# Attention and bilinear FFN on one core: later batches' q·kv as block-diagonal full-array products, dummy products spread over the first batch, g turned later

## The chip, the cores and the metric

One core of one Trainium2 chip. The metric is the device time of one execution in microseconds (us). Every run also has a span (first to last instruction in the trace) and a mean granted clock of TensorE. The time is the span plus 1.8 us (for example 330.38 and 328.6). A difference of under 2% counts as "same". Ratios are the mean time of one kernel's fast runs over that of the other's of the same rounds, so they are not quite the ratio of the medians that are quoted beside them. I call an execution near its kernel's lowest time a *good draw*, and one 1.4 us or more above it a *bad draw*.

Engines: PE is TensorE (products), PEld its weight loads, DVE is VectorE, ACT is ScalarE, POOL is GpSimd, SP is SyncE.

## The reference

```python
# q, k, v: (batch 8, heads 8, seq 576, dim 64), fp32
kv  = einsum('bhsd,bhse->bhde', k, v)          # 64x64 per head
o   = einsum('bhsd,bhde->bhse', q, kv)
x   = o / sqrt(mean(o*o, -1) + 1e-6) * g_norm  # then (4608 tokens) x 512
out = ((x @ w_a) * (x @ w_b)) @ w_out          # w_a, w_b: 512x1536, w_out: 1536x512
```

## The kernel before

The FFN works on strips of 512 tokens: 12 units of eight 128x128x512 products (four with w_a, four with w_b), then four output blocks of twelve products. This is the bulk of TensorE's work. The attention of batch b+1 is put into *slots* between the units of strip b. Batch 0 has nothing to hide behind and runs first, pair of heads by pair of heads, with dummy products of zeros to keep TensorE busy. Two heads (64 rows each) share the 128 partitions.

```python
    def kv(self, p, o):                     # two heads: halves of the columns
        for c in range(EC):                 # EC = 6 pieces of 96 tokens
            for j in range(2):
                nc.tensor.matmul(o[j * D : (j + 1) * D, :],
                    lhsT=kt[..][:, self.head(p, j), c, :], rhs=vt[..][:, self.head(p, j), c, :], ...)

    def head(self, p, j):                   # later batches pair head p with head p + 4
        return 2 * p + j if self.b < EARLY else p + j * NP

    def x(self, m, h, i0):                  # later batches: four 64x64 products, all quadrants
        ts = slice(h * HF, (h + 1) * HF)    # HF = 288 tokens
        for j, c in ((0, 0), (1, 1), (0, 1), (1, 0)):
            r = slice(j * D, (j + 1) * D)
            nc.tensor.matmul(P[c * D : (c + 1) * D, i0 + j, 0:HF],
                lhsT=self.kvs[r, 2 * m + c, :], rhs=self.qT[r, 2 * m + c, ts], ...)
        nc.scalar.activation(sq[(2 * m + h) % 3], P[:, i0 : i0 + 2, 0:HF], AF.Square)

    # ss: two products ones (128x128) x sq (288 columns), ACT rsqrt, DVE writes xt
    ...
    # the first batch
    dummy(10, 0)                            # 128x128x512 products of zeros
    A.qtr(0, 2)                             # transposes of q on TensorE
    A.qtr_out(0, 2)
    nc.tensor.matmul(P[:, 6, 0:1], lhsT=g_row, rhs=one, start=True, stop=True)
    nc.vector.tensor_copy(g_col, P[:, 6, 0:1])
    dummy(2, 7)
    A.kv1(0, 3)
    A.kv1_out(0, 3, nc.vector.tensor_copy)
    for p in range(NP - 1):
        A.qtr(p + 1, ..)                    # next pair's transposes
        A.qtr_out(p + 1, ..)
        if p: A.pst(p - 1, ..)              # DVE: xt of the pair before
        A.px(p, i)                          # q.kv, quadrants on the diagonal
        A.psq(p, i)                         # ACT: square
        A.kv1(p + 1, ..)
        dummy(1, 7)
        A.pss(p, SS)                        # sum of squares, ACT: rsqrt
        A.kv1_out(p + 1, ..)
    ...
    # slots: in each strip four x, each followed one unit later by its ss
```

## Time and profile before

| | before |
|---|---|
| time, first three timed runs | 327.41 us median (327.39 to 327.51) |
| the profiled execution | 330.38 us, span 328.6 |
| PE busy | 320.3 us, 97% of the span |
| x slots | 6 batches x 4 |

The profiled execution is 3 us slower than the timed ones.

The page of the kernel before, its first parts. PEclk is the granted clock in tenths, one digit for each fortieth of the span:

```profile
span 328.6 us, 4913 instructions
PE 320.3 (97%) x1962; PEld 148.4 (45%) x1997; DVE 123.6 (38%) x213; ACT 122.5 (37%) x206; POOL 60.0 (18%) x82
...
PEclk9999999999999999999999999999999999999999
...
PE 95%; DMA 2%; issue 1%; DVE 1%; ACT 1%; ACTq 0%
```

TensorE is what ends last (95% of the chain of waits). ACT and DVE have more than half their time free.

The PE timeline of before around one x slot. Columns: start in us, length in us, engine, line, operation, operands, rows and columns of the array, columns streamed, count:

```profile
66.95 1.03 PE L260 MATMUL P<-xt,wb_t 128*128 128x512 bf16 x4
67.91 0.32 PE L219 MATMUL P<-qT,kvs 64*64 64x288 bf16 x4
68.16 1.04 PE L260 MATMUL P<-xt,wa_t 128*128 128x512 bf16 x4
69.03 1.03 PE L260 MATMUL P<-xt,wb_t 128*128 128x512 bf16 x4
69.89 0.41 PE L231 MATMUL P<-sq,ones 128*128 128x288 bf16 x2
70.14 1.03 PE L260 MATMUL P<-xt,wa_t 128*128 128x512 bf16 x4
```

Lengths include the pipeline, so read starts. Undisturbed, four products of 512 columns take 0.863 us, 0.2158 each. From 66.95 to 69.03 there are eight of them (1.73 us) in 2.08 us: the x slot between them costs 0.35 us. From 69.03 to 70.14 there are four (0.86) in 1.11: the sum-of-squares slot costs 0.25 us, though it streams twice 288 columns where the four quadrants, all started within 10 ns, stream 288 once.

The PE timeline of before in the first batch:

```profile
1.19 4.45 PE L329 MATMUL P<-zeros 128*128 128x512 bf16 x10 [1.19 <-DVE eps_t L344]
...
9.15 0.69 PE L164 MATMUL P<-ident,qt 96*64 96x96 bf16 x12 [0.32 <-DVE kvs L158]
...
11.87 0.69 PE L164 MATMUL P<-ident,qt 96*64 96x96 bf16 x12
...
14.59 0.69 PE L164 MATMUL P<-ident,qt 96*64 96x96 bf16 x12
...
17.95 0.38 PE L260 MATMUL P<-xt,wa_t 128*128 128x512 bf16 x1 [0.16 <-issue]
...
19.19 0.38 PE L260 MATMUL P<-xt,wa_t 128*128 128x512 bf16 x1 [0.30 <-DVE xt L205]
```

Ten dummies in 4.45 us are 0.427 apart, double the 0.2158 of later: TensorE is at half rate. The clock's own record says so too: it has full rate from 17.456 us for 310.613 us, and nothing before. (310.613 is 91 times 3.413 us; that length is called a *window* below.) The row PEclk of the page still shows 9 in its first slices; stretches without a record read as full there. A pair of heads takes 2.72 us (9.15, 11.87, 14.59).

### The profile page before, as it was taken

How to read it: one execution, taken by the hardware profiler on the slowest of the kernel's cores; microseconds unless marked ns; L12 is line 12 of the kernel's file. 1: busy time of each engine (PE TensorE's matmuls, PEld its weight loads, DVE VectorE, ACT ScalarE, POOL GpSimd, SP SyncE). 2: the span in 40 equal slices, each digit the busy share in tenths (PEclk: the TensorE clock that was granted, in tenths of full speed). 3: DMA queues.
4: the chain of work that ended last, by engine and by line, in shares of the span. 5: the costliest groups of instructions: out<-in, count | busy, mean ns of one | idle time of the engine just before them, and what ended most of it. 6: DMA issues, size and time to landing. Idle time of an engine off the chain costs nothing.

```text
span 328.6 us, 4913 instructions
## 1 busy us (share of the span) xinstructions
PE 320.3 (97%) x1962; PEld 148.4 (45%) x1997; DVE 123.6 (38%) x213; ACT 122.5 (37%) x206; POOL 60.0 (18%) x82
## 2 busy tenths in 40 slices
PE   7999999999999999999999999999999999999995
PEld 3544454444444444444444444444444444444443
DVE  2453325444234432443245323642345234304421
ACT  3353234444234433553254324532354243223310
POOL 8945860410014050410060000000000000000000
PEclk9999999999999999999999999999999999999999
DMA  8999999791359999693599032002000200021002
GB/s 179 197 196 200 200 195 236 100 171 27 98 104 132 157 125 223 84 171 87 145 62 156 34 110 60 0 21 92 17 0 2 96 32 3 0 97 33 0 32 96
DMA packets 70043, 32.61 MB, mean 99 GB/s; under 512 B 43652, under 2 KB 65540, under 8 KB 70020
## 3 DMA queue, kind: packets, MB, share of 16 engines
q0 software_dynamic: 49712, 18.44, 47.4%
q1 hardware_dynamic: 19952, 13.50, 16.0%
q10 hardware_dynamic: 356, 0.36, 0.4%
q8 instruction: 15, 0.25, 0.3%
q14 instruction: 8, 0.07, 0.1%
HBM read 37.75 MB, written 12.98 MB: 154 GB/s over the span
## 4 chain that ended last, share of the span: by engine, by line
PE 95%; DMA 2%; issue 1%; DVE 1%; ACT 1%; ACTq 0%
PE P L260 57%; PE P L304 28%; PE P L142 2%; PE P L219 2%; PE P L231 2%; DMA g_row<-in_g_norm_dram 1%; PE P L164 1%; PE P L178 1%; PE P L191 1%; PE P L329 1%; DMA out_dram<-osb 1%; DVE xt L205 0%; ACT rs L195 0%; DVE osb L319 0%; ACT sq L187 0%
## 5 line engine op out<-in xcount | busy, mean ns | idle before, releaser
L276 DVE TENSOR_TENSOR ab<-P,asb 128x512 bf16<-128x512 f32 x108 | 74.5, 691 | 126.6 <-PE P L260 125.7
L260 PE MATMUL P<-xt,wb_t 128*128 128x512 bf16 x430 | 111.4, 379 | 0.4
L260 PE MATMUL P<-xt,wa_t 128*128 128x512 bf16 x410 | 109.6, 380 | 1.3 <-DVE xt L205 0.3
L304 PE MATMUL P<-wo_t,ab 128*128 128x512 bf16 (+1 forms) x434 | 97.1, 373 | 0.7 <-issue 0.3
L274 ACT CAST asb<-P 128x512 bf16<-128x512 f32 x108 | 63.0, 585 | 88.5 <-PE P L260 87.7
L260 PEld LDWEIGHTS <-wb_t 128*128 128x128 bf16 x432 | 42.3, 98 | 51.3 <-issue 0.5
L304 PEld LDWEIGHTS <-ab 128*128 128x128 bf16 x444 | 42.3, 98 | 46.2 <-issue 0.2
L260 PEld LDWEIGHTS <-wa_t 128*128 128x128 bf16 x432 | 40.1, 98 | 44.9 <-issue 0.2
L239 DVE SCALAR_TENSOR_TENSOR xt<-P,g_col,rs 128x288 bf16<-128x288 f32 x48 | 22.6, 513 | 19.6 <-ACT rs L234 19.6
L317 ACT COPY osb<-P 128x512 f32<-128x512 f32 x17 | 10.0, 585 | 49.3 <-PE P L304 47.5
L319 DVE COPY osb<-P 128x512 f32<-128x512 f32 x18 | 12.4, 692 | 33.0 <-PE P L304 33.0
L234 ACT ACTIVATE rs<-P,eps_t 128x576 f32<-128x576 f32 x24 | 17.8, 741 | 16.6 <-PE P L231 16.6
L226 ACT ACTIVATE sq<-P 128x576 bf16<-128x576 f32 x24 | 15.6, 651 | 18.3 <-PE P L219 18.3
L118 POOL DMA_DIRECT2D qs<-in_q_dram x12 | 19.3, 1819 | 2.0 <-issue 1.9
L115 POOL COPY gate<-qT 1x1 bf16<-1x1 bf16 x5 | 0.9, 176 | 98.0 <-DMA qT<-qs 98.0
L95 POOL DMA_DIRECT2D vt<-in_v_dram x13 | 14.7, 1132 | 0.9 <-DMA qt<-in_q_dram 0.6
L95 POOL DMA_DIRECT2D kt<-in_k_dram x13 | 14.8, 1142 | 0.1
L142 PEld LDWEIGHTS <-kt 96*64 96x64 bf16 x384 | 8.1, 117 | 6.4 <-issue 6.4
L205 DVE SCALAR_TENSOR_TENSOR xt<-P,g_col,rs 128x288 bf16<-128x288 f32 x16 | 7.6, 513 | 6.8 <-ACT rs L195 6.8
L142 PE MATMUL P<-vt,kt 96*64 96x64 bf16 x384 | 10.0, 203 | 0.0
L231 PE MATMUL P<-sq,ones 128*128 128x288 bf16 x48 | 9.8, 286 | 0.0
L195 ACT ACTIVATE rs<-P,eps_t 128x576 f32<-128x576 f32 (+1 forms) x9 | 6.2, 687 | 6.9 <-PE P L191 6.9
(47 smaller groups left out, 85.4 us busy)
## 6 DMA issues: line engine op xcount, KB each, us to landing
out_dram<-osb SPq DMA_DIRECT2D x23, 256.0 KB, 2.0
qs<-in_q_dram POOLq DMA_DIRECT2D x12, 288.0 KB, 7.5
kt<-in_k_dram POOLq DMA_DIRECT2D x6, 576.0 KB, 10.2
vt<-in_v_dram POOLq DMA_DIRECT2D x6, 576.0 KB, 12.6
out_dram<-osb SPq DMA_DIRECT2D x13, 128.0 KB, 2.3
wo_t<-in_moe_w_out_dram POOLq DMA_DIRECT2D x12, 128.0 KB, 6.0
wa_t<-in_moe_w_a_dram POOLq DMA_DIRECT2D x5, 256.0 KB, 9.1
wb_t<-in_moe_w_b_dram POOLq DMA_DIRECT2D x5, 256.0 KB, 9.7
```

What stands on the lines that cost most here:

```text
L95: nc.gpsimd.dma_start(out=t[:, hs, :, :], in_=src[b, hs].rearrange("h (t c) d -> t h c d", c=EC))
L118: nc.gpsimd.dma_start(out=d[:, :, j, :], in_=q[b, j * NP : (j + 1) * NP].rearrange("h t d -> t h d"),)
L142: nc.tensor.matmul(o[j * D : (j + 1) * D, :], lhsT=kt[self.b % NB][:, self.head(p, j), c, :], rhs=vt[self.b % NB][:, self.head(p, j), c, : ...
L226: nc.scalar.activation(sq[(2 * m + h) % 3], P[:, i0 : i0 + 2, 0:HF], AF.Square)
L231: nc.tensor.matmul(P[:, i0 + j, 0:HF], lhsT=ones, rhs=sq[n][:, j, :], start=True, stop=True)
L234: nc.scalar.activation(rs[n], P[:, i0 : i0 + 2, 0:HF], AF.Abs_reciprocal_sqrt, bias=eps_t)
L239: nc.vector.scalar_tensor_tensor(out=xt[m + 2 * j][:, t0 : t0 + HF], in0=P[:, x0 + j, 0:HF], scalar=g_col, in1=rs[n][:, j, :], op0=ALU.mul ...
L260: nc.tensor.matmul(self.a if w is wa_t else self.b, lhsT=w[:, kc, self.fc * 128 : (self.fc + 1) * 128], rhs=xt[kc][:, t0 : t0 + STRIP], st ...
L274: nc.scalar.copy(self.t, self.a)
L276: nc.vector.tensor_mul(abt[self.s % 2][self.fc], self.b, self.t)
L304: nc.tensor.matmul(P[:, i, e0:e1], lhsT=abt[s % 2][fc][:, g * 128 : (g + 1) * 128], rhs=wo_t[:, fc, e0:e1], start=(fc == 0), stop=(fc == F ...
L319: nc.vector.tensor_copy(t, P[:, i, :])
```

## The change

The intent, in two halves. In later batches, two heads' kv (64x64 each) go on the diagonal of a 128x128 tile whose other two blocks are zero; one product of 128 rows then gives both heads, without switching the array to 64x64 tiles. Heads 2p and 2p+1 are now paired throughout, which changes how q is laid down. In the first batch, 11 and 4 dummies instead of 10 and 2 run before the first kv, five more are spread over the loop, and g is turned into a column after the first x instead of before the first kv.

```diff
+    kvb = [sb([128, NP, 128], BF16, f"kvb{i}") for i in range(2)]   # zeroed once by DVE
...
-        d = qs_d[b].rearrange("t (p j d) -> t p j d", p=NP, j=2)
-        for j in range(2): ... d[:, :, j, :] <- q[b, j * NP : (j + 1) * NP]
+        d = qs_d[b].rearrange("t (h d) -> t h d", h=H)
+        for hs in (slice(0, NP), slice(NP, H)): ... d[:, hs, :] <- q[b, hs]
...
-        def kv_out(self, p0, p1, src):
-            nc.scalar.copy(self.kvs[:, p0:p1, :], src)
+        def kv_out(self, src):
+            for j in range(2):
+                r = slice(j * D, (j + 1) * D)
+                nc.scalar.copy(kvb[self.b % 2][r, :, r], src[r])
...
-        def x(self, m, h, i0):  ... four 64x64 products (above)
+        def x(self, p, i0):
+            for h in range(2):
+                nc.tensor.matmul(P[:, i0 + h, 0:HF], lhsT=kvb[self.b % 2][:, p, :],
+                    rhs=self.qT[:, p, h * HF : (h + 1) * HF], start=True, stop=True)
...
-    dummy(10, 0)
+    dummy(11, 0)
     A.qtr(0, 2)
     A.qtr_out(0, 2)
-    nc.tensor.matmul(P[:, 6, 0:1], lhsT=g_row, rhs=one, start=True, stop=True)
-    nc.vector.tensor_copy(g_col, P[:, 6, 0:1])
-    dummy(2, 7)
+    dummy(4, 7)
...                                          # in the loop over pairs
         A.psq(p, i)
+        if p == 0:
+            nc.tensor.matmul(P[:, 1, 0:1], lhsT=g_row, rhs=one, start=True, stop=True)
+            nc.vector.tensor_copy(g_col, P[:, 1, 0:1])
+        dummy(1, 2 + p % 2)
         A.kv1(p + 1, 2 + p % 2)
         dummy(1, 7)
         A.pss(p, SS)
         A.kv1_out(p + 1, 2 + p % 2, nc.vector.tensor_copy)
+        if p < NP - 2:
+            dummy(1, 2 + (p + 1) % 2)
```

More of the change, by code (lines that the diff above doesn't have):

```diff
@@ L115, in load_late @@
             nc.gpsimd.tensor_copy(gate, qT[(b - 1) % 2][0:1, 0, 0:1])
-        d = qs_d[b].rearrange("t (p j d) -> t p j d", p=NP, j=2)
-        for j in range(2):
-            nc.gpsimd.dma_start(
-                out=d[:, :, j, :],
-                in_=q[b, j * NP : (j + 1) * NP].rearrange("h t d -> t h d"),
-            )
+        d = qs_d[b].rearrange("t (h d) -> t h d", h=H)
+        for hs in (slice(0, NP), slice(NP, H)):
+            nc.gpsimd.dma_start(out=d[:, hs, :], in_=q[b, hs].rearrange("h t d -> t h d"))
         load_heads(b, kt[b % NB], k, slice(0, H))
@@ L133, in __init__ @@
             self.qT = qT[b % 2]
-        def head(self, p, j):
-            return 2 * p + j if self.b < EARLY else p + j * NP
         def kv(self, p, o):
@@ L143, in kv @@
                         o[j * D : (j + 1) * D, :],
-                        lhsT=kt[self.b % NB][:, self.head(p, j), c, :],
-                        rhs=vt[self.b % NB][:, self.head(p, j), c, :],
+                        lhsT=kt[self.b % NB][:, 2 * p + j, c, :],
+                        rhs=vt[self.b % NB][:, 2 * p + j, c, :],
                         start=(c == 0),
@@ L165, in qtr @@
                         t[j * D : (j + 1) * D, c, :],
-                        qt[self.b][:, self.head(p, j), c, :],
+                        qt[self.b][:, 2 * p + j, c, :],
                         ident[0:EP, 0:EP],
@@ L212, in pst @@
                 )
-        def x(self, m, h, i0):
-            ts = slice(h * HF, (h + 1) * HF)
-            for j, c in ((0, 0), (1, 1), (0, 1), (1, 0)):
-                r = slice(j * D, (j + 1) * D)
+        def x(self, p, i0):
+            for h in range(2):
                 nc.tensor.matmul(
-                    P[c * D : (c + 1) * D, i0 + j, 0:HF],
-                    lhsT=self.kvs[r, 2 * m + c, :],
-                    rhs=self.qT[r, 2 * m + c, ts],
+                    P[:, i0 + h, 0:HF],
+                    lhsT=kvb[self.b % 2][:, p, :],
+                    rhs=self.qT[:, p, h * HF : (h + 1) * HF],
                     start=True,
                     stop=True,
-                )
-            nc.scalar.activation(sq[(2 * m + h) % 3], P[:, i0 : i0 + 2, 0:HF], AF.Square)
-        def ss(self, m, h, i0, x0):
-            n = (2 * m + h) % 3
-            for j in range(2):
-                nc.tensor.matmul(
-                    P[:, i0 + j, 0:HF], lhsT=ones, rhs=sq[n][:, j, :], start=True, stop=True
-                )
-            nc.scalar.activation(
-                rs[n], P[:, i0 : i0 + 2, 0:HF], AF.Abs_reciprocal_sqrt, bias=eps_t
-            )
-            t0 = self.b * S + h * HF
-            for j in range(2):
-                nc.vector.scalar_tensor_tensor(
-                    out=xt[m + 2 * j][:, t0 : t0 + HF],
-                    in0=P[:, x0 + j, 0:HF],
-                    scalar=g_col,
-                    in1=rs[n][:, j, :],
-                    op0=ALU.mult,
-                    op1=ALU.mult,
                 )
@@ L347 @@
     nc.vector.memset(ones, 0.0)
+    for t in kvb:
+        nc.vector.memset(t, 0.0)
     nc.vector.memset(ones[0:D, 0:D], 1.0 / D)
@@ L447, in slot @@
             if n == k0 + kn - 1:
-                A.kv_out(0, NP, kb)
-        for i, (m, h) in enumerate(((0, 0), (1, 0), (0, 1), (1, 1))):
-            if n == xs[i]:
-                A.x(m, h, X[0])
-            if n == xs[i] + 1:
-                A.ss(m, h, SS, X[0])
+                A.kv_out(kb)
+        for p in range(NP):
+            if n == xs[p]:
+                A.x(p, X[0])
+                A.psq(p, X[0])
+            if n == xs[p] + 1:
+                A.pss(p, SS)
+                A.pst(p, X[0])
     for s in range(1, N_STRIP - 1):
```

## The prediction

> **What bounds the kernel now.** TensorE: busy 320.3 of 328.6 us in the engine table, 95% of the chain of waits. After the first batch, PE work is critical one for one. Two parts are touched.
>
> 1. Later batches (six, four x slots each). In the timeline at 67.9 us four 64x64 products of 288 columns start within 10 ns (all four quadrants at once), but the stream stops on both sides: last full product at 67.600, second one after the slot at 68.384. Less two steps of 0.216 that is 0.352 us a slot. The sum-of-squares slot, two full 128x128 products of 288 columns, steps by 0.122 us without a break: 0.247 us. The Trainium skill, "TensorEngine Tiling (Array Packing)", Key Properties, says a change of tiling mode drains TensorE; the trace agrees.
>
> 2. First batch (0 to 18 us). 512-column dummies step by 0.427 us until 17.2 us, later products by 0.216. The clock record of full speed starts at 17.456 us and lasts 310.613, 91 times 3.413. The Trainium skill, "TensorE: Matmul & The Clock Gate", Part 1, has a free-running window of 3413 ns that must be busy before TensorE leaves half rate. So the whole first batch runs at half rate, one pair per 2.72 us (transposes at 9.15, 11.87, 14.59 us).
>
> **What the change does.**
> - x: 16 quadrant products per batch become 8 full ones, shaped like the sum-of-squares ones. Estimate: 0.352 - 0.247 = 0.105 us, times 24 slots = -2.5 us, all on PE. ACT gets one more kv copy per batch (about 0.37 us) and has room (37% busy); DVE's two memsets fit before the first loads land. The new q layout should cost nothing.
> - Dummies: 11, the transposes and 4 more make 6.9 us of unbroken work from 1.19 us at half rate, over two windows, so one whole window fits at any phase. I expect full rate from about 7 us, kept by the dummies in the loop. Moving g takes about 0.5 us out of the path to the first kv.
> - At full rate the ACT chain sets the pair's period: square 0.65, rsqrt 0.74, and the turn over PE, about 0.6 to 0.7: 2.0 to 2.2 us. With the first x product 1 us earlier I estimate the dense part 2.3 us sooner. The loads cap it: batch 1's first k/v pair landed 3.7 us before its use.
>
> Sum: -2.5 - 2.3, about -4.8 us.
>
> **Prediction:** 322.6 us, 8 in 10 between 320.5 and 325.2. Faster by over 2% (below 320.9): 0.14; within 2%: 0.85; slower: 0.01.
>
> **What would show it.** (a) Each later x group: two products 0.12 us apart, no break around them; a strip's period from 34.6 to about 34.2 us. (b) The full-speed clock record begins near 7 us. (c) First-batch pairs every 2.1 us with PE waiting for ACT's square; the third unit's products (21.90 us before) begin near 19.5. (d) Little PE waiting on loads.
>
> **What would make it wrong.** Timed runs are 3 us below the profiled one, so before may already reach full rate earlier when timed; then the first batch gives little. Products of zeros may not count as activity: then five extra dummies in the loop cost about 2 us. Or the first batch gains over 3.7 us and then stalls on loads. Or x slots wait for DVE's buffer release, which already held one slot per strip (0.15 us at 77.74 us).

## The result, and the profile after

| | before | after |
|---|---|---|
| first measurement, median | 327.46 us (4 runs, 327.39 to 327.51) | 324.82 us (3 fast runs, 324.81 to 325.27); 325.04 with the run of 854.88 counted |
| ratio | | 0.9924, 95% interval 0.9905 to 0.9944 |
| measured again, median | 327.65 us (11 runs, 327.08 to 330.10) | 324.86 us (6 runs, 324.80 to 325.70) |
| ratio | | 0.9898, 0.9864 to 0.9931 |
| mean of those runs | 328.33 us | 325.04 us |

The change is faster by 0.8 to 1.0%, within the 2% that counts as the same. The range of the prediction held the result, but near its slow end: 2.6 us were won by the medians of fast runs (2.8 when measured again) and not 4.8. That is not the whole mechanism confirmed: one of the two terms of the sum is not in the timed runs at all, as shown below, and the range was wide enough to hold the result without it.

One of the four runs of the changed kernel in the first measurement took 854.88 us, and it was the profiled one. Products of 512 columns were 0.621 us apart in most cases and 0.485 in about one of five, neither the half nor the full rate seen elsewhere (the 0.587 of an expectation below is a mean over a stretch of them), and its clock table was empty. None of the other nine runs of this kernel did this. It is a slow run and explains nothing here; the profile below is of the changed kernel run again unaltered (run after_again, span 323.0).

The page of the changed kernel, in that repeat:

```profile
span 323.0 us, 4853 instructions
PE 316.9 (98%) x1957; PEld 150.9 (47%) x1957; DVE 124.1 (38%) x215; ACT 124.7 (39%) x212; POOL 60.2 (19%) x82
...
PE 96%; DMA 2%; DVE 1%; ACT 0%; issue 0%; ACTq 0%
```

Its PE timeline around the same x slot:

```profile
64.03 1.03 PE L234 MATMUL P<-xt,wb_t 128*128 128x512 bf16 x4
64.89 0.41 PE L214 MATMUL P<-qT,kvb 128*128 128x288 bf16 x2
65.14 1.03 PE L234 MATMUL P<-xt,wa_t 128*128 128x512 bf16 x4
66.00 1.03 PE L234 MATMUL P<-xt,wb_t 128*128 128x512 bf16 x4
```

Eight products of 512 columns and the slot now take 66.00 - 64.03 = 1.97 us: the slot costs 0.25 us, like the sum-of-squares slot, and the 0.1 us of silence ahead of it (67.81 to 67.91 before) is gone.

Its PE timeline in the first batch:

```profile
1.19 3.84 PE L303 MATMUL P<-zeros 128*128 128x512 bf16 x11 [1.19 <-DVE eps_t L318]
5.79 0.45 PE L161 MATMUL P<-ident,qt 96*64 96x96 bf16 x12 [0.76 <-DVE qt L344]
...
7.84 0.45 PE L161 MATMUL P<-ident,qt 96*64 96x96 bf16 x12 [0.32 <-DVE kvs L155]
...
10.30 0.45 PE L161 MATMUL P<-ident,qt 96*64 96x96 bf16 x12
...
12.45 0.45 PE L161 MATMUL P<-ident,qt 96*64 96x96 bf16 x12
...
16.26 0.38 PE L234 MATMUL P<-xt,wa_t 128*128 128x512 bf16 x1 [0.31 <-DVE xt L202]
16.48 0.38 PE L234 MATMUL P<-xt,wb_t 128*128 128x512 bf16 x1
...
18.98 1.03 PE L234 MATMUL P<-xt,wa_t 128*128 128x512 bf16 x4
```

Full rate begins at 3.853 us by the clock record, and the pairs take 2.46 and 2.15 us (7.84, 10.30, 12.45) instead of 2.72. The product that waits for DVE's xt stands at 16.26 us instead of 19.19. Against the profile of before this is 2.9 us sooner, the 2.3 us and more that was forecast. But the timed runs do not show it. So the two profiles do not compare what the timed runs compare.

### The profile page after: what moved, and what is told of

Same layout as the page of the kernel before. It is cut to its first block, busy times and chain, and to the rows that moved or that the text cites. A ratio compares the mean times of both kernels' runs of the same rounds, so it can differ in the third digit from the quotient of the medians.

```text
span 853.1 us, 4818 instructions
## 1 busy us (share of the span) xinstructions
PE 835.1 (98%) x1922; PEld 267.5 (31%) x1957; DVE 124.7 (15%) x215; ACT 126.0 (15%) x212; POOL 60.4 (7%) x82
## 4 chain that ended last, share of the span: by engine, by line
PE 96%; issue 2%; DMA 1%; POOL 0%; DVE 0%; ACT 0%; POOLq 0%
PE P L234 59%; PE P L278 30%; PE P L188 3%; PE P L214 2%; PE P L137 2%; DMA qt<-in_q_dram 1%; DMA wb_t<-in_moe_w_b_dram 1%; PE P L175 1%; PE P L161 0%; PE P L303 0%; POOL wa_t L331 0%; POOL vt L96 0%; DVE osb L473 0%; POOL ident masks.py:199 0%; ACT osb L471 0%
## 5 line engine op out<-in xcount | busy, mean ns | idle before, releaser
L234 PE MATMUL P<-xt,wb_t 128*128 128x512 bf16 x422 | 279.8, 834 | 3.4 <-issue 3.4
L234 PE MATMUL P<-xt,wa_t 128*128 128x512 bf16 x419 | 277.6, 834 | 5.2 <-issue 5.2
L278 PE MATMUL P<-wo_t,ab 128*128 128x512 bf16 (+1 forms) x434 | 258.9, 817 | 3.6 <-issue 3.6
L234 PEld LDWEIGHTS <-wb_t 128*128 128x128 bf16 x432 | 73.9, 171 | 181.6 <-issue 181.1
L278 PEld LDWEIGHTS <-ab 128*128 128x128 bf16 x444 | 77.0, 174 | 166.1 <-issue 163.2
L234 PEld LDWEIGHTS <-wa_t 128*128 128x128 bf16 x432 | 74.7, 175 | 156.0 <-issue 155.2
L192 ACT ACTIVATE rs<-P,eps_t 128x576 f32<-128x576 f32 (+1 forms) x33 | 24.0, 726 | 89.9 <-PE P L188 82.6
L188 PE MATMUL P<-sq,ones 128*128 128x288 bf16 x64 | 29.8, 582 | 0.0
L214 PE MATMUL P<-qT,kvb 128*128 128x288 bf16 x48 | 21.9, 579 | 0.0
L303 PE MATMUL P<-zeros 128*128 128x512 bf16 x21 | 13.2, 773 | 1.2 <-DVE eps_t L318 1.2
```

The source lines that it names most:

```text
L188: nc.tensor.matmul(P[:, i0 + h, 0:HF], lhsT=ones, rhs=sq[p % 3][:, h, :], start=True, stop=True)
L192: nc.scalar.activation(rs[p % 3][:, h0:h1, :], P[:, i0 + h0 : i0 + h1, 0:HF], AF.Abs_reciprocal_sqrt, bias=eps_t,)
L214: nc.tensor.matmul(P[:, i0 + h, 0:HF], lhsT=kvb[self.b % 2][:, p, :], rhs=self.qT[:, p, h * HF : (h + 1) * HF], start=True, stop=True,)
L234: nc.tensor.matmul(self.a if w is wa_t else self.b, lhsT=w[:, kc, self.fc * 128 : (self.fc + 1) * 128], rhs=xt[kc][:, t0 : t0 + STRIP], st ...
L278: nc.tensor.matmul(P[:, i, e0:e1], lhsT=abt[s % 2][fc][:, g * 128 : (g + 1) * 128], rhs=wo_t[:, fc, e0:e1], start=(fc == 0), stop=(fc == F ...
L303: nc.tensor.matmul(P[:, i, 0:cols], lhsT=zeros[:, 0:128], rhs=zeros[:, 0:cols], start=True, stop=True)
```

## The experiments

Twelve runs, all correct. Nine are in the table; the other three are more profiles of the kernel before.

| run | x | front (dummies, g) | dummies added in the loop | median us (range) | runs 1.5 us or more above the lowest | full rate from, in the profile |
|---|---|---|---|---|---|---|
| before_again | quadrants | 10, g, 2 | no | 328.42 (327.45 to 330.41) | 3 of 6 | 6.13 us |
| after_again | full | 11, 4, g later | yes | 324.86 (324.80 to 325.70) | 0 of 6 | 3.85 us |
| x_only | full | 10, g, 2 | no | 325.57 (324.69 to 327.11) | 3 of 6 | 6.48 us |
| first_only | quadrants | 11, 4, g later | yes | 327.50 (327.46 to 327.71) | 0 of 6 | 5.21 us |
| front_only | full | 11, 4, g later | no | 324.66 (324.45 to 324.74) | 0 of 6 | 4.07 us |
| loop_only | full | 10, g, 2 | yes | 325.60 (324.68 to 327.79) | 3 of 6 | 6.66 us |
| front_early | full | 11, 4, g later | no | 324.54 (324.51 to 324.70) | 0 of 6 | 4.98 us |
| quad_pairs | halves on the diagonal | 11, 4, g later | yes | 330.12 (330.00 to 330.42) | 0 of 6 | 4.63 us |
| no_dummies | full | none, g later | none at all | 327.36 (326.78 to 327.83) | 0 of 6 | 18.83 us |

The first four ran on one chip with 11 runs of before (327.08 to 330.10), front_only to quad_pairs on a second with 11 (327.40 to 330.38), no_dummies on a third with 11 (327.30 to 330.14).

Theory A: x pays all of the gain; the dummies bring full rate, but the timed runs of before mostly had it already. Theory B: the dummies pay, x does not.

### after_again, before_again: the two kernels unaltered

> The changed kernel unaltered, for a profile in the fast state (the one on hand shows TensorE stepping 512 columns every 0.587 us for the whole span, and 853 us). Theory A (the products pay, the dummies bring full rate but the timed runs of the kernel before already had it): each later x slot costs 0.247 us on the stream instead of 0.352, 2.5 us in all, and full rate begins near 7 us. Theory B (the dummies pay, the x slots do not): x slots still cost about 0.35 us. Ratio to before 0.992 either way.

> The kernel before unaltered, for a second profile. If the profiled execution on hand reached full rate late by chance of the window's phase, this one starts its full-rate record at another time (for example 10.6 or 14.0 us) with a span 1.5 to 3 us shorter than 328.6; if it is a property of the kernel, again near 17.5 us and 328.6. Ratio 1.000.

Ratio of after_again 0.9898 (0.9864 to 0.9931), of before_again 1.0009 (0.9967 to 1.0052). The profile of before_again has a span of 325.7 us, 2.9 us less than the first profile of the same kernel. Its PE timeline in the first batch:

```profile
1.20 4.45 PE L329 MATMUL P<-zeros 128*128 128x512 bf16 x10 [1.20 <-DVE eps_t L344]
...
7.90 0.45 PE L164 MATMUL P<-ident,qt 96*64 96x96 bf16 x12 [0.32 <-DVE kvs L158]
...
9.79 0.45 PE L164 MATMUL P<-ident,qt 96*64 96x96 bf16 x12
...
11.80 0.45 PE L164 MATMUL P<-ident,qt 96*64 96x96 bf16 x12
...
15.56 0.38 PE L260 MATMUL P<-xt,wa_t 128*128 128x512 bf16 x1 [0.26 <-DVE xt L205]
16.46 0.39 PE L260 MATMUL P<-xt,wb_t 128*128 128x512 bf16 x1 [0.52 <-DMA wb_t<-in_moe_w_b_dram]
...
18.98 1.03 PE L260 MATMUL P<-xt,wa_t 128*128 128x512 bf16 x4
```

Full rate from 6.128 us, pairs every 1.89 to 2.01 us, and then TensorE waits for the second w_b block, which landed at 16.41 us by the trace. The changed kernel's product with that block stands at 16.48 us. There the block landed at 16.39, but the wait that ended last was for DVE's xt, at 16.26; with an earlier xt that product could have come less than 0.1 us sooner before it met the load. The last lines of the two timelines settle it: the third unit of the first strip starts at 18.98 us in both. So in a good draw the first batch has next to nothing to give. The first profile of before was a bad draw.

### x_only, first_only: the change in two halves

The edits are the diff above, split: x_only takes everything but the lines of the first batch, first_only takes those alone.

> Only the full 128-row products in the later batches; the first batch is as in the kernel before. Theory A: 2.5 us faster than before, ratio 0.992, so the same as the whole change. Theory B: within 0.5 us of before. If both halves pay and something takes half back, about 2.5 us faster here and also faster in the other half.

> Only the spread dummies and the later g; x in quadrant products as before. Theory A: within 0.5 us of before, ratio 0.9985 to 1.0015, though the profile shows full rate from about 7 us. Theory B: 2.5 us faster. If products of zeros do not count as activity: full rate not before 17 us and 1 to 2 us slower.

x_only: ratio 0.9917 (0.9878 to 0.9956). first_only: 0.9973 (0.9938 to 1.0009). The full products win 327.50 - 324.86 = 2.64 us (first_only to after_again, medians, both without bad draws), which is 0.110 us for each of 24 slots; 0.105 was forecast. The good draws of x_only and of before in the same rounds say the same, 324.72 against 327.45 by their medians. The other half does not move the good runs (lowest 327.46, before's good runs 327.08 to 327.65) but it takes the bad draws away: three of six in x_only are 1.5 to 2.4 us above its lowest, none in first_only is more than 0.3. In means, 328.33 of before falls by 2.66 in x_only and by 0.80 in first_only, together 3.46; the whole change has 3.29. (The 0.80 alone is not clear of noise, the interval of first_only reaches 1.0009. That bad draws go with the front is clear only over all runs, see below.) Theory A stands and Theory B falls, but A's claim that first_only has no effect holds for the median only.

### front_only, loop_only: which dummies

```diff
# front_only, against the change
-        dummy(1, 2 + p % 2)
...
-        if p < NP - 2:
-            dummy(1, 2 + (p + 1) % 2)
# loop_only, against the change
-    dummy(11, 0)
+    dummy(10, 0)
...
-    dummy(4, 7)
+    nc.tensor.matmul(P[:, 6, 0:1], lhsT=g_row, rhs=one, start=True, stop=True)
+    nc.vector.tensor_copy(g_col, P[:, 6, 0:1])
+    dummy(2, 7)
...
-        if p == 0: (g, in the loop)
```

> The whole change without the five dummies inside the first batch's loop; the 11 and 4 in front and the later g stay. Each kernel so far has runs near its lowest time and, where the loop has no extra dummies, about half the runs 1.5 to 3 us above it. Theory F (the unbroken front brings full rate at any phase and that is enough): all runs within 1 us of 324.8. Theory L (the gaps inside the loop let TensorE fall back to half rate, whatever the front does): some of six runs at 326 to 327.5 with a mean granted clock below 0.995.

> The whole change with the front as before (10 dummies, g, 2 dummies) but the five dummies in the loop kept. Theory L: all runs within 1 us of 324.8. Theory F: some of six runs 1.5 us or more above that.

front_only: ratio 0.9868 (0.9833 to 0.9902), six runs within 0.29 us. loop_only: 0.9910 (0.9866 to 0.9955), with runs at 326.26, 327.64 and 327.79. Theory F holds: the unbroken front does it, and the added dummies in the loop protect nothing that shows. (One dummy a pair, which the kernel before has too, stays in both.) They may cost a little: front_only's median is 0.2 us below the change's, but on different chips, so this is not shown. Nor do the runs separate the three edits of the front, one dummy more, then two more, and g moved away.

### no_dummies: what the dummies are worth at all

```diff
# against front_only
-    dummy(11, 0)
-    dummy(4, 7)
-        dummy(1, 7)
```

> front_only without any dummy. If the front dummies are what brings full rate before the first batch, TensorE starts it at half rate in every run here: pairs about 2.3 to 2.7 us apart, full rate only when the dense first strip has filled a window, near 18 to 22 us, and all six runs 3 to 5 us above front_only (327.5 to 329.5), with none near 324.7. If the transposes and kv products were enough by themselves, within 0.5 us of 324.7.

Ratio 0.9965 (0.9931 to 0.9999); 2.70 us above front_only by the medians, on different chips, a little less than the least that was expected. The PE timeline of no_dummies:

```profile
10.63 0.69 PE L161 MATMUL P<-ident,qt 96*64 96x96 bf16 x12
...
13.25 0.69 PE L161 MATMUL P<-ident,qt 96*64 96x96 bf16 x12
...
18.41 0.59 PE L234 MATMUL P<-xt,wa_t 128*128 128x512 bf16 x1
18.83 0.38 PE L234 MATMUL P<-xt,wb_t 128*128 128x512 bf16 x1
```

Half rate until 18.832 us, a pair every 2.62 us. This course is much like the first profile of before. All six runs lie within 1.1 us and none is near 324.7, so it is probably the usual course of this kernel; only one of them was profiled. TensorE here had transposes and products all the way from 5.78 us with no idle stretch over 0.4 us by the profile, and stayed at half rate for 13 us.

### quad_pairs: is it the full array, or the new head order?

```diff
# against the change
-                    P[:, i0 + h, 0:HF],
-                    lhsT=kvb[self.b % 2][:, p, :],
-                    rhs=self.qT[:, p, h * HF : (h + 1) * HF],
+                for j in range(2):
+                    r = slice(j * D, (j + 1) * D)
+                        P[r, i0 + h, 0:HF], lhsT=kvb[self.b % 2][r, p, r], rhs=self.qT[r, p, ...]
```

> The whole change, but each x product is split into its two 64x64 halves on the diagonal (same head order, same kv tile, same columns in all). Theory drain (a switch to 64x64 tiles stops the stream, about 0.23 us per slot, worked out as 0.352 less one run of 288 columns, 0.122): a slot costs about 0.47 us instead of 0.247, 24 slots add 5.4 us, about 330.3, slower even than before. Rival (the gain came from the head order or the q layout, or quadrant products are no dearer in themselves): within 0.5 us of the whole change.

Ratio 1.0037 (0.9998 to 1.0075). The PE timeline of quad_pairs at the same slot:

```profile
64.01 1.03 PE L236 MATMUL P<-xt,wb_t 128*128 128x512 bf16 x4
64.97 0.43 PE L216 MATMUL P<-qT,kvb 64*64 64x288 bf16 x4
65.33 1.04 PE L236 MATMUL P<-xt,wa_t 128*128 128x512 bf16 x4
66.20 1.03 PE L236 MATMUL P<-xt,wb_t 128*128 128x512 bf16 x4
```

66.20 - 64.01 less eight steps is 0.47 us for the slot; 330.12 - 324.86 = 5.26 us (on different chips), or 0.22 for each of 24 slots (5.4 expected). Head order, q layout, kv copies and columns streamed are those of the change, so what the full array takes away is the switch into 64x64 tiles and back, 0.22 us a time. By the starts in the trace 0.09 of it lies ahead of the first tile product, 0.11 behind the last, and 0.02 between the two halves of tokens (0.146 us apart instead of 0.122). In the stream of full products a weight load starts with the product before its own; at the switch it starts only at 64.96, with its own product. Whether the emptying of the array or the late weight load takes the time is not separated. The quadrants of the kernel before paid it too (0.23: a slot of 0.35 less one run of 288 columns, 0.12), but streamed all four at once and so got half of it back. That is why the gain was 0.11 and not 0.22.

### front_early: is the load what the first strip waits for?

```diff
# against front_only: first weight blocks of 128 columns, then 128, then 256 as before
-    WC = 256
+    WC = 128
...
-    for i in range(1, d_ff // WC):
-        load_ab(i * WC, (i + 1) * WC)
+    load_ab(WC, 2 * WC)
+    for i in range(1, d_ff // (2 * WC)):
+        load_ab(i * 2 * WC, (i + 1) * 2 * WC)
```

> As front_only, with the first weight blocks of 128 columns instead of 256, so the weights of the first unit are asked for in half the bytes. If in good runs the first strip starts when the second wb block lands (16.4 us) and not when the dummies or ACT let it, this is 0.4 to 0.8 us faster than front_only's good runs, near 324.2, and the third unit starts near 18.3 us. If the first batch's own chain sets the start, no difference (under 0.2 us).

Ratio 0.9866 (0.9832 to 0.9900), median 0.12 us below front_only's. That total is what was expected if the first batch's own chain set the start (under 0.2 us), but the trace shows that it was the load, and that the lead is lost later. The PE timeline of front_only, then of front_early, at the start of the first strip:

```profile
14.98 0.29 PE L188 MATMUL P<-sq,ones 128*128 128x288 bf16 x1
15.87 0.39 PE L234 MATMUL P<-xt,wa_t 128*128 128x512 bf16 x1 [0.60 <-DMA wa_t<-in_moe_w_a_dram]
16.38 0.39 PE L234 MATMUL P<-xt,wb_t 128*128 128x512 bf16 x1
```

```profile
14.99 0.29 PE L188 MATMUL P<-sq,ones 128*128 128x288 bf16 x1
15.54 0.38 PE L234 MATMUL P<-xt,wa_t 128*128 128x512 bf16 x1 [0.26 <-DVE xt L202]
15.75 0.38 PE L234 MATMUL P<-xt,wb_t 128*128 128x512 bf16 x1
```

The wait on the load is gone and the same product comes 0.63 us sooner (15.75 for 16.38). Later starts, in us from the trace:

| | front_only | front_early | lead |
|---|---|---|---|
| third unit of the first strip | 18.89 | 18.25 | 0.64 |
| first output product | 35.95 | 35.30 | 0.65 |
| kv of batch 1, first pair | 40.38 (v landed 39.73) | 39.73 (v landed 39.85) | 0.65 |
| kv of batch 1, last pair | 47.85 (v landed 47.12) | 47.48 (v landed 47.61) | 0.37 |
| kv of batch 2 | 60.46 | 60.25 | 0.21 |

(Below the first row the starts are those of weight loads. The weight load of k runs ahead of the wait for v; the products themselves start at 39.89 and 47.66 us in front_early.) The lead is given back at batch 1's loads. In front_only v lands 0.65 and 0.73 us before the kv of the first and last pair, in front_early after the first weights of k are in, and the products wait for it. Behind the first wait for loads stands a second, so no more than about 0.2 us are left of the lead (0.21 at batch 2, 0.12 in the medians).

### phase_a, phase_b, phase_c: more profiles of before

> The kernel before once more, one profile at a chance phase of the clock window. Either full rate from one of the windows' ends near 4 to 7.3 us on and a span near 325.7, or one of two slower courses: full rate reached early, lost in the gaps of the first batch for two or three windows of 3.41 us and regained (mean granted clock 0.984 to 0.989, span 327 to 328.4), or not reached before 17 us (span 328.6).

> The kernel before again, a second draw of the phase, with the same alternatives: full rate kept from 4 to 7.3 us on (span near 325.7), reached early and lost again for two or three windows (clock 0.984 to 0.989, span 327 to 328.4), or not reached before 17 us (span 328.6).

> The kernel before, a third draw of the window's phase. In 33 timed runs of it about half had 327.1 to 328.2 us and half 328.5 to 330.4, many of the latter with a mean granted clock of 0.984 to 0.99. If this draw is of that kind, the clock table should show full rate beginning about 5 to 6 us, a half-rate stretch of two or three windows (6.8 or 10.2 us) beginning about 9 us, and full rate again; if not, a span near 325.7 with one full-rate record from 4 to 7.3 us on.

All three were good draws: 327.68, 327.56 and 327.57 us, full rate from 6.757, 5.349 and 3.965 us. In all 47 timed runs of before, 20 were over 328.4 us. Several of the slow ones have a mean granted clock of 0.984 to 0.990, which the first profile (0.999) does not have: two or three windows of 3.41 us at half rate after full rate had been recorded would give this (3 x 3.413 / 2 is 1.6% of 328). That these runs reach full rate in the front and lose it in the gap before the first kv is argued, not shown; no profile caught one.

## Why the prediction was right or wrong

**The x slots: right in mechanism and size.** Forecast -2.5 us, measured -2.64. The slot fell from 0.35 to 0.25 us. The Trainium skill, "TensorEngine Tiling (Array Packing)", Key Properties, says that a change of tiling mode drains TensorE; quad_pairs put the number to it, 0.22 us there and back. ACT's extra kv copy (12 copies of 0.366 us for 6 of 0.372) and the memsets cost nothing that shows.

**The first batch: wrong.** The step that failed is "So the whole first batch runs at half rate", and with it "I estimate the dense part 2.3 us sooner". That was read correctly from one execution, and it was not the execution that the time is about. The profiled run took 330.38 us and the timed ones 327.4, and the 1.8 us between time and span were there to be seen (330.38 against 328.6), so the timed spans had to be near 325.6. In these, full rate comes by 4 to 7 us in the kernel before as well (before_again and three more profiles). There the first strip cannot go on before the second w_b block lands, at 16.4 us in both kernels, and its third unit starts at 18.98 us in both: 0 us sooner and not 2.3. The prediction named the doubt ("before may already reach full rate earlier when timed") and still put -2.3 in the sum.

**What the dummies do instead.** They take away the bad draws. The first measurement had four good draws of before, by luck (20 of 47 were bad), so the median saw nothing of it; over 11 runs the mean falls by 0.80 us (first_only). A bad run of before (up to 330.4) against first_only (327.5) is worth 2.9 us, so the size was about right for the draw that had been profiled.

**"One whole window fits at any phase": supported.** All 33 fast runs of the five kernels with the 11-and-4 front stay within 0.9 us of their kernel's lowest. Each of the kernels with the 10, g, 2 front has bad draws. In the bad draw that was profiled, windows end at 3.80 and 7.22 us (17.456 less steps of 3.413); TensorE starts at 1.19, and around g the front has gaps, so that I estimate 76 and 62% of these two windows were filled with streamed columns (0.427 us for 512). **"Kept by the dummies in the loop": wrong.** front_only keeps full rate without them, loop_only has bad draws with them.

**g: not separated.** "About 0.5 us out of the path" was forecast. The first kv starts at 7.14 us in after_again and at 7.21 in before_again (6.91 to 7.58 in all six profiled good draws of the old front), but two more dummies stand there now, 0.43 us at full rate, and take back what moving g gives. The third unit shows that nothing of it reaches the total.

**The load cap: right that there is one, wrong which.** The forecast had 3.7 us of room before batch 1's loads. In a good draw the room was 0.85 us (before_again: v landed at 39.61, kv began at 40.46), and the first weight block binds before that.

## What to carry to other kernels

Before a gain is worked out from a profile, check that the profiled run is a typical one: compare its time with the timed runs, and with the clock's record of when full rate begins. Here a short run of nearly unbroken products at the start, about two clock windows long at half rate, bought reproducible full rate; added dummies afterwards were not needed. Small products that switch the array's tiling in the middle of a stream of full ones can be dearer than full ones half filled with zeros (0.35 us against 0.25 here): count the switch, not the columns.

## What the Trainium skill lacked or had wrong

- "TensorE: Matmul & The Clock Gate", section "Why this matters for your kernels", asks for TensorE to be kept busy for 4 us or more continuously to reach full rate. How busy a window must be is not said, and busy time in the profile does not tell: in no_dummies the window from 8.59 to 12.01 us is busy all through by the profile and did not bring full rate. Columns streamed tell more. As an estimate (0.427 us for 512 columns at half rate, windows counted back in steps of 3.413 from each record's start), in the 13 profiles that have a clock record the window before full rate was filled to 75% or more, and the earlier ones to 76% or less (43, 65 and 60% in no_dummies after 5.18 us, then 80). Transposes are among the 75%: without them it would be 61 (phase_a), and 76% of dummies did not suffice (before, first profile).
- The same page, Part 1, does not say whether products of zeros count as activity. They do: at 3.853 us after_again had run nothing else and full rate began.
- The window of 3413 ns in Part 1 agrees with the traces: full-rate records last, for example, 310.613, 317.440 and 320.853 us, which are 91, 93 and 94 windows. It also says that the same kernel's slow start varies with the window's phase, and puts the loss under 1% of a typical span. Here the kernel before, in 47 runs, spread from 327.1 to 330.4 us, 1.0%, which is as much as the change won.
- The same page, section "Back-to-back issue gap", gives 131 ns per product of 512 columns as the sustained rate with weight loads. Here it is 216 ns, with a weight load for each, hundreds of times.
- "TensorEngine Tiling (Array Packing)", Key Properties, gives no figure for the drain: 0.20 to 0.23 us here, to 64x64 tiles and back.
- No page explains the 854.88 us run, with steps of 0.621 and 0.485 us per 512 columns for the whole execution; its cause stays open.
